# Turning K on VectorE in 32x32 blocks instead of on TensorE, in a decode-attention kernel

## Chip, cores, metric

One NeuronCore of a Trainium2 chip, one launch. The metric is device time in microseconds. The profiled executions give the span, which is about 2 us shorter than that time.

## The reference, cut to what matters

```python
# A: one query token, 32 heads, 4 KV heads, 65,536 cached keys of 128 numbers, bf16
q = (x @ wq).reshape(1, 1, 32, 128)
scores = einsum("bhqd,bhkd->bhqk", q, repeat(k_cache, 8)) * 128 ** -0.5
o = einsum("bhqk,bhkd->bhqd", softmax(scores), repeat(v_cache, 8))
A = o.reshape(1, 1, 4096) @ wo
# B: a small MLP on the same token (w1, w2: 1024x1024; w3: 1024x3584; w4: 3584x1024)
out = x + A + B
```

Almost all bytes are the two caches: 67 MB each of 170 MB. Every byte is used for one token, so there is little arithmetic per byte.

## The kernel before

The caches are cut into 16 units of 16,384 keys. One unit is one K tile and one V tile of 128 partitions x 16,384 bf16 (4.19 MB each). All big loads go through one queue in a fixed order into five rotating buffers; a load is issued when a buffer comes free.

```python
stream = [("wq", 0), ("wq", 1), ("K", 0), ("K", 1), ("V", 0), ("w3", 0), ("w3", 1)]
for u in range(2, NU):
    stream += [("K", u), ("V", u - 1)]
    ...                                   # w1, w2, wo go through one smaller slot
stream += [("V", NU - 1), ("wo", HKV - 1), ("w4", 0), ("w4", 1)]
```

Keys lie on partitions, but the scores contract over the 128 numbers of a key; both kernels turn K for that. Before, TensorE did it, on bf16 pairs read as 4-byte words; VectorE and ScalarE brought the result back to SBUF:

```python
def k_bank(u, b):                         # 16 banks per K tile
    for a in range(4):
        nc.tensor.transpose(pt[:, 128*a:128*(a+1)], words[...], ident_f[:])
    eng = nc.scalar.copy if evac[0] % ACT_EVERY == 0 else nc.vector.tensor_copy
    eng(out=kt[:, 1024*b:1024*(b+1)], in_=pt[:].bitcast(BF16))

def k_scores(u, sub, s):                  # queries padded to 32 columns, four column strips
    for i in range(4):
        for r in range(2):
            nc.tensor.matmul(sc[32*i:32*(i+1), :], lhsT=qpad[:, g, s, r, :],
                             rhs=cols[:, sub, s, :, 32*i:32*(i+1), r], ..., tile_position=(0, 32*i))
    ...                                   # VectorE: scale, maximum; later ScalarE: exp
```

P is then turned by VectorE (`pT`), multiplied with V (`oacc`), and per group of four units merged (`og`, `pm_e`). The end of the program is this:

```python
    compute_w4(0)      # 32 matmuls into psB
    flush()            # the last wo projection: 16 matmuls
    compute_w4(1)      # 24 matmuls
    # cast, then the output is written
```

## Time and profile before

| | before |
|---|---|
| median time | 409.7 us (3 runs, 409.57 to 410.14) |
| busy: PE / DVE / ACT | 275.4 / 207.1 / 108.7 us |
| bytes read | 169.88 MB |

The page of the profile, parts 1 to 3: busy times of the engines; then, in 40 slices of the span, the busy share of the 16 DMA engines in tenths and the rate; then DMA queues as packets, MB and share of all DMA time.

```profile
PE 275.4 (68%) x2420; PEld 196.5 (48%) x2420; DVE 207.1 (51%) x452; ACT 108.7 (27%) x162; POOL 4.6 (1%) x18
...
DMA  8999999999999999999999999999999999999991
GB/s 358 416 444 430 418 425 439 413 424 448 415 444 428 427 416 440 441 423 425 433 438 427 425 422 443 424 428 433 433 435 427 411 451 425 433 420 433 438 402 76
...
q1 hardware_dynamic: 6772, 169.87, 97.5%
q8 instruction: 19, 0.31, 0.3%
q14 instruction: 7, 0.06, 0.0%
```

No engine is near full, but the DMA row is at 9 (90% or more) from the second slice to the last but one. Queue q1 holds the loads. The two "instruction" queues carry the fetches of the program itself: 26 packets, 0.37 MB, for 5706 instructions here. The page gives their share of the same 16 DMA engines (0.3% for q8).

The table of busy time by stretch, for nearly the whole span and for the end (columns: from:to, length, busy time of each engine, granted TensorE clock, DMA share, GB/s):

```profile
4.00:390.00 386.00, 266.06 (x2348) 193.23 (x2349) 206.45 (x451) 107.24 (x160) 2.83 (x5) 0.85 1.00 429
...
396.00:398.00 2.00, 2.00 (x18) 0.69 (x14) 0.00 (x0) 0.00 (x0) 0.00 (x0) 0.77 0.78 317
398.00:400.00 2.00, 2.00 (x22) 0.76 (x18) 0.00 (x0) 0.00 (x0) 0.00 (x0) 1.00 0.56 213
400.00:402.00 2.00, 2.00 (x22) 0.78 (x20) 0.00 (x0) 0.00 (x0) 0.00 (x0) 1.00 0.10 37
```

For 386 us the DMA share is 1.00 at 429 GB/s. At the end the share does not drop at once (0.78, 0.56, 0.10): some DMA engines finish later than others. The sixteen landings that the first part of w4 counts are spread from 389.52 to 394.10 us in the trace's records. The costliest groups of the parts to be replaced (line, engine, operation, output<-inputs, shapes, count | busy, mean ns of one | idle before, and what ended it):

```profile
L366 PE MATMUL ptk<-ident_f,big 128*128 128x128 f32 x1024 | 156.9, 317 | 53.3 <-DMA big<-in_A_k_cache_dram 51.9
...
L370 DVE COPY big<-ptk 128x1024 bf16<-128x1024 bf16 x192 | 126.5, 687 | 83.2 <-PE ptk L366 82.9
L370 ACT COPY big<-ptk 128x1024 bf16<-128x1024 bf16 x64 | 64.7, 1012 | 163.8 <-PE ptk L366 163.7
L381 PE MATMUL sc<-big,qpad 128*32 128x512 bf16 x512 | 42.4, 394 | 17.4 <-ACT big L370 16.5
```

And the end of the chain of waits, in order of time (start us, us, what):

```profile
353.95 40.14 DMA big<-in_B_w_dram
394.14 9.32 PE psB L173 x67
403.48 0.68 DVE out_t L524
```

The first part of w4 lands at 394.14 us. From then on TensorE works through 72 queued matmuls (the chain names 67), and the output follows. The page's chain as a whole also names PE transposes (18% of the span). Those pieces lie where the chain passes through the freeing of a K buffer, while the DMA row beside them is full.

### The profile page before, as it was taken

What the parts mean: (1) busy time and instruction counts of PE and PEld (TensorE: products, weight loads), DVE (VectorE), ACT (ScalarE), POOL (GpSimd) and SP (SyncE); (2) the same over time, 40 slices, a digit from 0 to 9 for tenths busy, and PEclk for the clock granted to TensorE, in tenths of its full rate; (3) what the DMA queues carried; (4) which work ended last, traced back from release to release, by engine and by line L of the source; (5) the groups of instructions that cost most, each with busy time, mean ns of one, the idle gap of its engine ahead of it and who ended that gap; (6) DMA issues with size and microseconds to landing.
All of it is one profiled execution on the core that took longest, in us unless ns stands there. A gap on an engine that the chain in (4) does not pass through costs nothing.

```text
span 407.1 us, 5706 instructions
## 1 busy us (share of the span) xinstructions
PE 275.4 (68%) x2420; PEld 196.5 (48%) x2420; DVE 207.1 (51%) x452; ACT 108.7 (27%) x162; POOL 4.6 (1%) x18
## 2 busy tenths in 40 slices
PE   0377882394677588685858684768695886868346
PEld 0237651272646475455555462646473755656122
DVE  0434771082366656465656393555566654656500
ACT  1011452135034123232322033141411331323100
POOL 1000001000000000000000000000000000000000
PEclk9996997599598959896969899797969696969859
DMA  8999999999999999999999999999999999999991
GB/s 358 416 444 430 418 425 439 413 424 448 415 444 428 427 416 440 441 423 425 433 438 427 425 422 443 424 428 433 433 435 427 411 451 425 433 420 433 438 402 76
DMA packets 7104, 170.27 MB, mean 418 GB/s; under 512 B 1054, under 2 KB 1058, under 8 KB 1446
## 3 DMA queue, kind: packets, MB, share of 16 engines
q1 hardware_dynamic: 6772, 169.87, 97.5%
q8 instruction: 19, 0.31, 0.3%
q14 instruction: 7, 0.06, 0.0%
q0 software_dynamic: 160, 0.02, 0.0%
q10 hardware_dynamic: 146, 0.00, 0.0%
HBM read 169.88 MB, written 0.01 MB: 417 GB/s over the span
## 4 chain that ended last, share of the span: by engine, by line
DMA 62%; PE 30%; DVE 3%; ACT 2%; another core or an unknown queue 1%; issue 1%; SPq 0%
DMA big<-in_A_k_cache_dram 52%; PE ptk L366 18%; DMA big<-in_B_w_dram 10%; PE sc L381 5%; PE psB L173 3%; PE oacc L441 3%; ACT big L370 2%; DVE og L461 1%; PE pm_e L472 1%; DVE big L370 1%; DVE og L459 0%; DVE pT L431 0%; PE pm_mx L403 0%; SPq L132 0%
## 5 line engine op out<-in xcount | busy, mean ns | idle before, releaser
L366 PE MATMUL ptk<-ident_f,big 128*128 128x128 f32 x1024 | 156.9, 317 | 53.3 <-DMA big<-in_A_k_cache_dram 51.9
L366 PEld LDWEIGHTS ptk<-ident_f,big 128*128 128x128 f32 x1024 | 139.9, 165 | 80.3 <-issue 77.3
L370 DVE COPY big<-ptk 128x1024 bf16<-128x1024 bf16 x192 | 126.5, 687 | 83.2 <-PE ptk L366 82.9
L370 ACT COPY big<-ptk 128x1024 bf16<-128x1024 bf16 x64 | 64.7, 1012 | 163.8 <-PE ptk L366 163.7
L381 PE MATMUL sc<-big,qpad 128*32 128x512 bf16 x512 | 42.4, 394 | 17.4 <-ACT big L370 16.5
L390 DVE TENSOR_SCALAR_CACHE_REDUCE s_sb<-sc 128x512 f32<-128x512 f32 x32 | 22.1, 691 | 24.2 <-PE sc L381 23.5
L441 PE MATMUL oacc<-big,pT 128*32 128x512 bf16 x512 | 32.4, 392 | 2.5 <-DMA big<-in_A_v_cache_dram 2.5
L431 DVE STREAM_TRANSPOSE pT<-p_sb 128x512 bf16<-128x512 bf16 x32 | 22.5, 708 | 15.9 <-ACT p_sb L428 15.9
L381 PEld LDWEIGHTS <-qpad 128*32 128x32 bf16 x512 | 12.6, 95 | 28.4 <-issue 18.3
L441 PEld LDWEIGHTS <-pT 128*32 128x32 bf16 x512 | 18.1, 98 | 13.3 <-DVE pT L431 2.5
L472 PE MATMUL pm_e<-og,selbig 128*128 128x128 f32 x32 | 7.8, 422 | 12.9 <-DVE og L461 12.9
L448 ACT COPY ob<-oacc 128x512 f32<-128x512 f32 x12 | 7.0, 585 | 29.9 <-PE oacc L441 29.9
L472 PEld LDWEIGHTS pm_e<-og,selbig 128*128 128x128 f32 x32 | 6.7, 308 | 15.3 <-DVE og L461 11.1
L173 PE MATMUL psB<-big,cols_h 128*1 128x512 bf16 x56 | 7.7, 437 | 5.9 <-DMA big<-in_B_w_dram 5.9
L244 PE MATMUL psh<-big,ln_rep_b 128*32 128x512 bf16 x56 | 5.5, 504 | 7.1 <-DMA big<-in_B_w_dram 7.1
L416 PE MATMUL pm_mx<-ident_f,rep 1*128 1x1 f32 x16 | 3.6, 223 | 9.4 <-DVE rep L408 9.4
L183 PE MATMUL pm_ln<-ln_rowsum_a,ones_f 128*128 128x1 f32 x2 | 0.6, 348 | 13.7 <-DVE ln_rowsum_a L181 13.7
L428 ACT ACTIVATE p_sb<-s_sb,nball_2276 128x512 bf16<-128x512 f32 x8 | 5.7, 714 | 14.5 <-DVE nball_2276 L422 14.5
L461 DVE SCALAR_TENSOR_TENSOR og<-ob,wb,og 128x512 f32<-128x512 f32 x12 | 9.0, 752 | 0.4
L428 ACT ACTIVATE p_sb<-s_sb,nball_1438 128x512 bf16<-128x512 f32 x8 | 5.7, 714 | 12.2 <-DVE nball_1438 L422 12.2
L428 ACT ACTIVATE p_sb<-s_sb,nball_3096 128x512 bf16<-128x512 f32 x8 | 5.7, 715 | 12.0 <-DVE nball_3096 L422 12.0
L416 PEld LDWEIGHTS pm_mx<-ident_f,rep 1*128 1x128 f32 x16 | 2.2, 139 | 12.8 <-DVE rep L408 12.5
(163 smaller groups left out, 111.9 us busy)
## 6 DMA issues: line engine op xcount, KB each, us to landing
big<-in_A_k_cache_dram SPq DMA_DIRECT2D x16, 4096.0 KB, 46.1
big<-in_A_v_cache_dram SPq DMA_DIRECT2D x16, 4096.0 KB, 40.0
big<-in_A_wq_dram SPq DMA_DIRECT2D x2, 4096.0 KB, 21.5
big<-in_B_w_dram SPq DMA_DIRECT2D x2, 3584.0 KB, 40.6
big<-in_B_w_dram SPq DMA_DIRECT2D x1, 4096.0 KB, 40.1
w_624<-in_B_w_dram SPq DMA_DIRECT2D x1, 2048.0 KB, 35.7
w_1109<-in_A_wo_dram SPq DMA_DIRECT2D x1, 2048.0 KB
w_1735<-in_B_w_dram SPq DMA_DIRECT2D x1, 2048.0 KB
```

Source lines behind the costliest of these rows:

```text
L173: nc.tensor.matmul(psB[32 * j:32 * j + 1, :], lhsT=lhsT, rhs=rhs, start=False, stop=False, tile_position=(0, 32 * j), skip_group_check=True)
L366: nc.tensor.transpose(pt[:, 128 * a:128 * (a + 1)], words[:, 512 * b + 128 * a:512 * b + 128 * (a + 1)], ident_f[:])
L370: eng(out=kt[:, 1024 * b:1024 * (b + 1)], in_=pt[:].bitcast(BF16))
L381: nc.tensor.matmul(sc[32 * i:32 * (i + 1), :], lhsT=qpad[:, g, s, r, :], rhs=cols[:, sub, s, :, 32 * i:32 * (i + 1), r], start=(s == 0 and ...
L390: nc.vector.tensor_scalar(out=s_sb[:], in0=sc[:], scalar1=SCALE, scalar2=None, op0=ALU.mult, op1=ALU.max, accum_out=unit[(u, "mx")][:, sub ...
L416: nc.tensor.transpose(pm[:, P:P + 1], unit.pop((u, "rep"))[0:1, :], ident_f[0:1, 0:1])
L428: nc.scalar.activation(out=p_sb[:], in_=s_sb[:], func=ACTF.Exp, bias=nball[:, b:b + 1], scale=1.0, accum_out=lsum[:, sub:sub + 1])
L431: nc.vector.transpose(out=pT[:], in_=p_sb[:])
L441: nc.tensor.matmul(oacc[32 * q:32 * (q + 1), :], lhsT=pT[:, 32 * t:32 * (t + 1)], rhs=vt[:, sub, :, t, :, :], start=(sub == 0 and t < 4), ...
L448: nc.scalar.copy(out=ob[:], in_=oacc[:])
L461: nc.vector.scalar_tensor_tensor(out=og[:], in0=ob[:], scalar=wb[:, k:k + 1], in1=og[:], op0=ALU.mult, op1=ALU.add)
L472: nc.tensor.matmul(pe[:, 0:P], lhsT=selbig[:, cg, :], rhs=og[:, 128 * cg:128 * (cg + 1)], start=(cg == 0), stop=(cg == 3))
```

## The change

The intent: VectorE's transpose, which the kernel before already uses on P (128x512 bf16, 0.71 us), is applied to the 4-byte words of K, in place. The changed kernel assumes that this turns 32x32 blocks and leaves the words of a key on 32 partitions of its own quadrant, four key groups side by side. Query weights that are block-diagonal over the four quadrants then give the scores with the full 128x128 array, and neither TensorE transposes of K nor their evictions remain.

```diff
-    def k_bank(u, b):
-        ... 4 TensorE transposes, 1 eviction on VectorE or ScalarE
+    def k_set(u, sub, s):                       # 8 sets per K tile
+        n = UKEYS // SUBS // SETS
+        at = (SETS * sub + s) * n
+        words = kt[:, at:at + n].bitcast(F32)   # 128 x 1024 words
+        nc.vector.transpose(out=words, in_=words)
+        k_scores(u, sub, s)

     def k_scores(u, sub, s):
-        for i in range(4):
+        for b in range(2):
             for r in range(2):
-                nc.tensor.matmul(sc[32*i:32*(i+1), :], lhsT=qpad[:, g, s, r, :],
-                                 rhs=cols[:, sub, s, :, 32*i:32*(i+1), r], ..., tile_position=(0, 32*i))
+                c0 = LEAD + P * (4 * g + 2 * b + r) - 8 * s
+                nc.tensor.matmul(sc[:], lhsT=qdiag[:, c0:c0 + P], rhs=cols[:, sub, s, :, b, :, r], ...)
@@ cut: query packing for qdiag, layout of V to match, PSUM: 2+2+2 banks instead of 4+1+1 @@
```

More of the change, by code (lines that the diff above doesn't have):

```diff
@@ L19 @@
 SUBS = 2
+SETS = 4
 BIG_BUFS = 5
-ACT_EVERY = 4
 W4_PIECES = (16, 8, 2, 1, 1)
@@ L55 @@
     SCALE = float(DH) ** -0.5
+    LEAD = 8 * (SETS - 1)
     const = ctx.enter_context(tc.tile_pool(name="const", bufs=1))
@@ L67 @@
     dram = ctx.enter_context(tc.tile_pool(name="dram", bufs=1, space=bass.MemoryType.DRAM))
-    ps_T = ctx.enter_context(tc.tile_pool(name="psT", bufs=4, space=bass.MemoryType.PSUM))
-    ps_S = ctx.enter_context(tc.tile_pool(name="psS", bufs=1, space=bass.MemoryType.PSUM))
-    ps_O = ctx.enter_context(tc.tile_pool(name="psO", bufs=1, space=bass.MemoryType.PSUM))
+    ps_T = ctx.enter_context(tc.tile_pool(name="psT", bufs=2, space=bass.MemoryType.PSUM))
+    ps_S = ctx.enter_context(tc.tile_pool(name="psS", bufs=2, space=bass.MemoryType.PSUM))
+    ps_O = ctx.enter_context(tc.tile_pool(name="psO", bufs=2, space=bass.MemoryType.PSUM))
     ps_M = ctx.enter_context(tc.tile_pool(name="psM", bufs=1, space=bass.MemoryType.PSUM))
@@ L157 @@
     nc.gpsimd.memset(eps_t[:], LN_EPS)
-    ones_f = const.tile([P, P], F32, name="ones_f")
+    ones_f = opool.tile([P, P], F32, name="ones_f", tag="ob")
     nc.gpsimd.memset(ones_f[:], 1.0)
@@ L164 @@
     nc.scalar.activation(out=warm_act[:], in_=eps_t[:], func=ACTF.Sqrt)
-    ident_bf = const.tile([P, P], BF16, name="ident_bf")
-    make_identity(nc, ident_bf[:])
-    qpad = const.tile([P, HKV, 2, 2, 32], BF16, name="qpad")
-    nc.gpsimd.memset(qpad[:], 0.0)
+    pick4 = const.tile([P, 4], BF16, name="pick4")
+    nc.gpsimd.tensor_copy(out=pick4[:], in_=ident_f[:, ::32])
+    spread = ogpool.tile([P, 4, P], BF16, name="spread", tag="og")
+    for b in range(2):
+        nc.gpsimd.tensor_copy(
+            out=spread[:, 2 * b:2 * b + 2, :].rearrange("p r (a i) -> p r a i", a=4),
+            in_=ident_f[:, 64 * b:64 * b + 64].rearrange("p (i r) -> p r i", r=2).unsqueeze(2).to_broadcast([P, 2, 4, 32]))
+    qdiag = const.tile([P, LEAD + HKV * 4 * P], BF16, name="qdiag")
+    nc.gpsimd.memset(qdiag[:], 0.0)
     psB = ps_B.tile([P, 512], F32, name="psB")
@@ L228 @@
     nc.vector.tensor_tensor(out=ln_s2[:], in0=negmean1[:], in1=rstd1[:], op=ALU.mult)
-    accx = tmp.tile([1, D], F32, name="accx", tag="t")
-    nc.vector.tensor_scalar(out=accx[:], in0=x_row[:], scalar1=ln_s1[0:1, 0:1], scalar2=ln_s2[0:1, 0:1],
-                            op0=ALU.mult, op1=ALU.add)
     for j in range(2):
-        nc.tensor.matmul(psB[32 * j:32 * j + 32, :], lhsT=first_row[0:1, :], rhs=accx[0:1, 512 * j:512 * (j + 1)],
+        accx = spool.tile([1, 512], F32, name="accx", tag="s_sb")
+        nc.vector.tensor_scalar(out=accx[:], in0=x_row[:, 512 * j:512 * (j + 1)], scalar1=ln_s1[0:1, 0:1],
+                                scalar2=ln_s2[0:1, 0:1], op0=ALU.mult, op1=ALU.add)
+        nc.tensor.matmul(psB[32 * j:32 * j + 32, :], lhsT=first_row[0:1, :], rhs=accx[0:1, :],
                          start=True, stop=False, tile_position=(0, 32 * j), skip_group_check=True)
@@ L262, in compute_wq @@
         del vals["psq"]
-        qpk = tmp.tile([P, 8, 2, 2, 64], BF16, name="qpk", tag="t")
-        for b in range(2):
-            for ts in range(2):
-                eng = nc.vector.tensor_copy if ts == 0 else nc.scalar.copy
-                eng(out=qpk[:, 4 * b:4 * b + 4, :, ts, :],
-                    in_=psq[b][:].rearrange("p (h j r) -> p h r j", h=4, r=2))
-        for r in range(2):
-            pt = ps_T.tile([P, 512], F32, name="ptq", tag="pt")
-            ptb = pt[:].bitcast(BF16).rearrange("p (h x) -> p h x", h=8)
-            for h in range(8):
-                nc.tensor.transpose(ptb[:, h, :], qpk[:, h, r, :, :].rearrange("p t j -> p (t j)"), ident_bf[:])
-            for s in range(2):
-                for ts in range(2):
-                    eng = nc.vector.tensor_copy if s == 0 else nc.scalar.copy
-                    eng(out=qpad[64 * ts:64 * ts + 64, :, s, r, 16 * s + 8 * ts:16 * s + 8 * ts + 8],
-                        in_=ptb[64 * ts:64 * ts + 64, :, ::32].rearrange("p h g -> p g h"))
+        q_row = tmp.tile([P, 2, 512], BF16, name="q_row", tag="t")
+        nc.vector.tensor_copy(out=q_row[:, 0, :], in_=psq[0][:])
+        nc.scalar.copy(out=q_row[:, 1, :], in_=psq[1][:])
+        pq = ps_M.tile([P, 5, 8 * HKV], F32, name="pm_q", tag="pm")
+        for h in range(8):
+            nc.tensor.matmul(pq[:, 4, :].rearrange("p (g h) -> p g h", h=8)[:, :, h],
+                             lhsT=q_row[:, h // 4, P * (h % 4):P * (h % 4 + 1)], rhs=pick4[:], start=True, stop=True)
+        qT = small.tile([P, 8 * HKV], BF16, name="qT")
+        nc.vector.tensor_copy(out=qT[:], in_=pq[:, 4, :])
+        for x in range(4):
+            nc.tensor.matmul(pq[:, x, :], lhsT=spread[:, x, :], rhs=qT[:], start=True, stop=True)
+        for a in range(4):
+            eng = nc.vector.tensor_copy if a % 2 == 0 else nc.scalar.copy
+            at = slice(32 * a, 32 * a + 32)
+            eng(out=qdiag[at, LEAD:].rearrange("p (g x c) -> p x g c", g=HKV, x=4)[:, :, :, 32 * a:32 * a + 8],
+                in_=pq[at, 0:4, :].rearrange("p x (g h) -> p x g h", h=8))
     def to_columns(rows, n, C, tag):
@@ L357 @@
     group = {}
-    evac = [0]
-    def k_bank(u, b):
+    def k_set(u, sub, s):
         kt = st.tiles[("K", u)]
-        words = kt[:].bitcast(F32)
-        pt = ps_T.tile([P, 512], F32, name="ptk", tag="pt")
-        for a in range(4):
-            nc.tensor.transpose(pt[:, 128 * a:128 * (a + 1)], words[:, 512 * b + 128 * a:512 * b + 128 * (a + 1)],
-                                ident_f[:])
-        evac[0] += 1
-        eng = nc.scalar.copy if evac[0] % ACT_EVERY == 0 else nc.vector.tensor_copy
-        eng(out=kt[:, 1024 * b:1024 * (b + 1)], in_=pt[:].bitcast(BF16))
+        n = UKEYS // SUBS // SETS
[3 more added lines that the diff above has]
+        k_scores(u, sub, s)
     def k_scores(u, sub, s):
-        g, b = divmod(u, NB)
+        g = u // NB
         kt = st.tiles[("K", u)]
-        cols = kt[:].rearrange("p (u s t k r) -> p u s t k r", u=SUBS, s=2, t=16, r=2)
+        cols = kt[:].rearrange("p (u s k b x r) -> p u s k b x r", u=SUBS, s=SETS, k=16, b=2, r=2)
         if s == 0:
@@ L378, in k_scores @@
         sc = unit[(u, "sc")]
-        for i in range(4):
+        for b in range(2):
             for r in range(2):
-                nc.tensor.matmul(sc[32 * i:32 * (i + 1), :], lhsT=qpad[:, g, s, r, :],
-                                 rhs=cols[:, sub, s, :, 32 * i:32 * (i + 1), r],
-                                 start=(s == 0 and r == 0), stop=(s == 1 and r == 1), tile_position=(0, 32 * i))
-        if s == 0:
+                c0 = LEAD + P * (4 * g + 2 * b + r) - 8 * s
+                nc.tensor.matmul(sc[:], lhsT=qdiag[:, c0:c0 + P], rhs=cols[:, sub, s, :, b, :, r],
+                                 start=(s == 0 and b == 0 and r == 0), stop=(s == SETS - 1 and b == 1 and r == 1))
+        if s < SETS - 1:
             return
@@ L388, in k_scores @@
             unit[(u, "ssb")] = []
-        s_sb = spool.tile([P, 512], F32, name="s_sb")
+        s_sb = spool.tile([P, 512], F32, name="s_sb", tag="s_sb")
         nc.vector.tensor_scalar(out=s_sb[:], in0=sc[:], scalar1=SCALE, scalar2=None, op0=ALU.mult, op1=ALU.max,
@@ L406, in max_row @@
                                 op=ALU.max, negate=True)
-        rep = small.tile([1, P], F32, name="rep")
+        rep = small.tile([1, P], F32, name="rep", bufs=1)
         nc.vector.tensor_copy(out=rep[:].rearrange("o (j h) -> o j h", h=8),
@@ L435, in compute_v @@
         g, b = divmod(u, NB)
-        vt = st.tiles[("V", u)][:].rearrange("p (u s t k d) -> p u s t k d", u=SUBS, s=2, t=16, k=2)
+        vt = st.tiles[("V", u)][:].rearrange("p (u s t d) -> p u s t d", u=SUBS, s=SETS, t=16)
         oacc = ps_O.tile([P, 512], F32, name="oacc")
@@ L441, in compute_v @@
                 nc.tensor.matmul(oacc[32 * q:32 * (q + 1), :], lhsT=pT[:, 32 * t:32 * (t + 1)],
-                                 rhs=vt[:, sub, :, t, :, :], start=(sub == 0 and t < 4),
+                                 rhs=vt[:, sub, :, t, :], start=(sub == 0 and t < 4),
                                  stop=(sub == SUBS - 1 and t >= 12), tile_position=(0, 32 * q))
@@ L453, in compute_v @@
         lall = group.pop((g, "lall"))
-        og = ogpool.tile([P, 512], F32, name="og")
+        og = ogpool.tile([P, 512], F32, name="og", tag="og")
         negmg = small.tile([P, 1], F32, name="negmg")
@@ L474, in group_rows @@
         nc.tensor.matmul(pe[:, P:P + 1], lhsT=sel8big[:], rhs=lp[:, 0:1], start=True, stop=True)
-        msk = small.tile([P, 16, 8], F32, name="msk")
+        msk = small.tile([P, 16, 8], F32, name="msk", bufs=1)
         nc.vector.tensor_tensor(out=msk[:], in0=pe[:, 0:P].rearrange("p (dd j) -> p dd j", j=8),
@@ L491, in group_project @@
         st.done(("wo", g))
-    BANKS = UKEYS // P // 8
     def compute_k(u):
-        for b in range(BANKS):
-            k_bank(u, b)
-            if b % 4 == 3:
-                after(2, lambda sub=b // 8, s=(b // 4) % 2: k_scores(u, sub, s))
-            tick()
+        for sub in range(SUBS):
+            for s in range(SETS):
+                k_set(u, sub, s)
+                tick()
     for it in stream:
```

## The prediction

> **What bounds the kernel now.** The DMA queue. The page's DMA table gives the load queue 97.5% of the 16 engines' span for 169.87 MB. The table of busy time by stretch shows DMA share 0.98 to 1.01 and 422 to 435 GB/s in every stretch from 4 us to 390 us, whether PE works (74% of 300 to 340 us: 430 GB/s) or not (4 to 10 us: 426). [...] A K load lands 46.1 us after issue (table of DMA issues): four to five tiles of 4.19 MB stand in the queue, so the queue never runs dry although the SP queue waits 220 us for DVE to free K buffers. Outside the load stream lie about 3 us of start and a tail: loads fade between 396 and 400 us, then 24 w4 matmuls (2.75 us), a cast (0.68 us), the output write, end at 407.1.
>
> The chain of waits names PE transposes (18%) and scores (5%), but beside a full DMA queue; they do not set the time.
>
> **Removed.** 1024 PE transposes (156.9 us busy), their PSUM evictions: 192 on DVE (126.5 us, 687 ns each) and 64 on ACT (64.7 us); 512 score matmuls on 32-column strips (42.4 us).
>
> **Added.** 128 DVE transposes in place of 128x1024 words. The trace's 128x512 bf16 transpose takes 0.71 us; [...] No run so far shows that a 4-byte element keeps that rate. And 512 full-array score matmuls over 512 columns: V's 32 strip matmuls run in 1.73 us, four side by side, so 0.216 us per 512 columns at full clock: estimate 111 us, up to twice that at half clock.
>
> **Balance.** DVE: 207 - 126.5 + 159, about 240 us (59%). PE: 275 - 199 + 111 to 160, about 190 to 235 us. ACT about 44 us. Per K+V pair the DMA needs 8.39 MB / 0.43 = 19.5 us; DVE needs 8 x 1.24 plus about 3.7 us of score eviction, P transposes and small work, about 13.6 us; PE some 9 to 14 us. Everything stays below the DMA.
>
> **On the critical path: nearly nothing.** The same bytes at the same rate, and the same tail, since PE idles before w4 in both. Predicted time 409.5 us, 80% range 406.5 to 412.5. Chances: faster by over 2% 0.02, within 2% 0.91, slower by over 2% 0.07.
>
> **What the profile would show.** Right: DMA queue again 97 to 98%, 415 to 421 GB/s mean; transposes near 1.24 us, DVE 56 to 62%, ACT near 11%, PE down to 45 to 60%; w4's first part still lands near 394 us. Transposes of about 2.3 us would refute the rate. A DMA share falling in mid-span would refute the bound.
>
> **What would make it wrong.** (1) 4-byte transposes at half rate: then DVE needs 8 x 2.3 + 3.7 = 22 us per pair, over the 19.5 of the DMA, and the time becomes some 415 to 425 us. (2) DVE's in-place traffic slowing DMA writes into the same memory; a 1% lower rate costs 4 us. (3) DVE's order: transposes of the next K behind a group merge that waits for V, draining the queue; 46 us of backlog should absorb it. (4) Faster than 402 us would need a load rate over 437 GB/s or no tail at all.

The step from the measured 0.71 us to the time of the new transpose came to 1.24 us each and 159 us for 128, the terms that stand under "Balance" (207 - 126.5 + 159, about 240 us; 8 x 1.24 + 3.7, about 13.6 us per pair); the 2.3 us for half rate rests on it too. These are guesses, for the run to test. The 409.5 us is the time before with the same loads and the same tail; the terms enter it only in that 13.6 us stays under the 19.5 us of the loads. The 437 GB/s of (4) works out as 169.87 MB in 402 us less about 13 us of start and tail.

## The result, and the profile after

| | before | after |
|---|---|---|
| median time | 409.68 us (4 runs, 409.57 to 410.14) | 408.75 us (4 runs, 407.91 to 408.94) |
| busy: PE / DVE / ACT | 275.4 / 207.1 / 108.7 us | 245.6 / 226.7 / 43.0 us |
| instructions | 5706 | 3502 |

The ratio is 0.9971, with a 95% interval of 0.9954 to 0.9989: the same at 2%, yet faster by a small amount that is clear of noise. Two later repeats gave 0.9969 and 0.9968. A ratio here is the mean time of one kernel's fast runs over that of the other's of the same rounds, so not quite the ratio of the medians quoted.

The same views of the changed kernel. The page, parts 1 to 3:

```profile
PE 245.6 (60%) x1392; PEld 97.6 (24%) x1392; DVE 226.7 (56%) x387; ACT 43.0 (11%) x95; POOL 6.4 (2%) x19
...
DMA  9999999999999999999999999999999999999991
GB/s 361 413 454 418 418 443 426 420 424 446 419 446 422 429 420 438 436 435 415 441 432 419 440 419 437 432 432 429 437 420 432 425 433 435 436 425 417 448 401 56
...
q1 hardware_dynamic: 6772, 169.87, 97.5%
q8 instruction: 11, 0.18, 0.2%
...
q14 instruction: 5, 0.04, 0.0%
```

Its table of busy time by stretch:

```profile
4.00:390.00 386.00, 235.51 (x1320) 94.20 (x1321) 226.04 (x386) 41.48 (x93) 2.95 (x6) 0.80 1.00 430
...
396.00:398.00 2.00, 2.00 (x14) 0.69 (x12) 0.00 (x0) 0.00 (x0) 0.00 (x0) 0.62 0.78 304
398.00:400.00 2.00, 2.00 (x22) 0.79 (x20) 0.00 (x0) 0.00 (x0) 0.00 (x0) 1.00 0.29 104
400.00:402.00 2.00, 2.00 (x22) 0.83 (x20) 0.00 (x0) 0.00 (x0) 0.00 (x0) 1.00 0.00 0
```

The groups that took the place of the four shown of the kernel before:

```profile
L387 PE MATMUL sc<-big,qdiag 128*128 128x512 bf16 x512 | 150.5, 457 | 82.5 <-DVE big L374 82.2
L374 DVE STREAM_TRANSPOSE big<-big 128x1024 f32<-128x1024 f32 x128 | 147.9, 1212 | 60.0 <-DMA big<-in_A_k_cache_dram 60.0
```

The end of its chain of waits:

```profile
350.62 42.39 DMA big<-in_B_w_dram
393.06 10.13 PE psB L182 x72
403.21 0.68 DVE out_t L526
```

What the reader should see: TensorE lost 30 us, ScalarE 66 us, VectorE gained 20 us, and the load queue did not notice: share 1.00, 430 GB/s instead of 429. VectorE now waits for K loads directly (60.0 us). The one difference on the path is at the end: the first part of w4 lands at 393.06 us, 1.08 us earlier (393.24 and 393.14 us in two repeats of the changed kernel), and the fade of the loads ends before 400 us instead of after it. Part of that is given back, because TensorE stayed at a granted clock of 0.50 longer in the tail (mean 0.62 instead of 0.77 from 396 to 398 us; the first 32 matmuls took 5.80 us instead of 4.98), so the two profiled spans differ by 0.3 us only, while the medians of the timed runs differ by 0.9 us.

### The profile page after: what moved, and what is told of

The parts are those of the page before. It is cut to its first block, busy times and chain, and to the rows that moved or that the text cites. A ratio compares the mean times of both kernels' runs of the same rounds, so it can differ in the third digit from the quotient of the medians.

```text
span 406.8 us, 3502 instructions
## 1 busy us (share of the span) xinstructions
PE 245.6 (60%) x1392; PEld 97.6 (24%) x1392; DVE 226.7 (56%) x387; ACT 43.0 (11%) x95; POOL 6.4 (2%) x19
## 3 DMA queue, kind: packets, MB, share of 16 engines
q1 hardware_dynamic: 6772, 169.87, 97.5%
## 4 chain that ended last, share of the span: by engine, by line
DMA 62%; PE 26%; DVE 10%; issue 1%; another core or an unknown queue 0%; SPq 0%; DVEq 0%
DMA big<-in_A_k_cache_dram 51%; PE sc L387 16%; DMA big<-in_B_w_dram 10%; DVE big L374 5%; PE oacc L446 4%; PE psB L182 3%; DVE s_sb L395 2%; DVE og L466 1%; PE pm_e L477 1%; PE pm_mx L408 0%; DVE pT L436 0%; DVE og L464 0%; PE pm_mx L421 0%; DVE rep L413 0%
## 5 line engine op out<-in xcount | busy, mean ns | idle before, releaser
L387 PE MATMUL sc<-big,qdiag 128*128 128x512 bf16 x512 | 150.5, 457 | 82.5 <-DVE big L374 82.2
L374 DVE STREAM_TRANSPOSE big<-big 128x1024 f32<-128x1024 f32 x128 | 147.9, 1212 | 60.0 <-DMA big<-in_A_k_cache_dram 60.0
L387 PEld LDWEIGHTS <-qdiag 128*128 128x128 bf16 x512 | 57.3, 112 | 175.7 <-issue 83.0
L446 PE MATMUL oacc<-big,pT 128*32 128x512 bf16 x512 | 42.9, 491 | 4.8 <-DMA big<-in_A_v_cache_dram 4.8
L395 DVE TENSOR_SCALAR_CACHE_REDUCE s_sb<-sc 128x512 f32<-128x512 f32 x32 | 21.6, 674 | 19.9 <-PE sc L387 19.9
L446 PEld LDWEIGHTS <-pT 128*32 128x32 bf16 x512 | 15.0, 115 | 22.2 <-issue 16.0
L408 PE MATMUL pm_mx<-ident_f,mxb 128*1 128x128 f32 x16 | 4.3, 269 | 16.6 <-DVE mxb L401 16.6
L182 PE MATMUL psB<-big,cols_h 128*1 128x512 bf16 x56 | 8.6, 472 | 5.3 <-DMA big<-in_B_w_dram 5.3
L192 PE MATMUL pm_ln<-ln_rowsum_a,ones_f 128*128 128x1 f32 x2 | 0.6, 348 | 13.6 <-DVE sel_180 L216 13.6
L464 DVE TENSOR_SCALAR og<-oacc,wb 128x512 f32<-128x512 f32 x4 | 3.0, 748 | 9.2 <-PE oacc L446 9.2
L481 DVE TENSOR_TENSOR msk<-pm_e,mask_188 128x128 f32<-128x128 f32 x4 | 1.2, 291 | 12.2 <-PE pm_e L479 12.2
```

The source lines that it names most:

```text
L182: nc.tensor.matmul(psB[32 * j:32 * j + 1, :], lhsT=lhsT, rhs=rhs, start=False, stop=False, tile_position=(0, 32 * j), skip_group_check=True)
L374: nc.vector.transpose(out=words, in_=words)
L387: nc.tensor.matmul(sc[:], lhsT=qdiag[:, c0:c0 + P], rhs=cols[:, sub, s, :, b, :, r], start=(s == 0 and b == 0 and r == 0), stop=(s == SETS ...
L395: nc.vector.tensor_scalar(out=s_sb[:], in0=sc[:], scalar1=SCALE, scalar2=None, op0=ALU.mult, op1=ALU.max, accum_out=unit[(u, "mx")][:, sub ...
L408: nc.tensor.transpose(pm[0:1, 0:P], unit.pop((u, "mxb"))[:, 0:1], ident_f[:])
L446: nc.tensor.matmul(oacc[32 * q:32 * (q + 1), :], lhsT=pT[:, 32 * t:32 * (t + 1)], rhs=vt[:, sub, :, t, :], start=(sub == 0 and t < 4), sto ...
```

## The experiments

One warning first. The comparison with the reference cannot vouch for attention in this problem. Kernels below that leave attention out altogether were also called correct, so its part of the output lies within the tolerance. That the changed layout is right was checked only by following its indices.

Theory: the load queue sets the time; all engine work of either kernel fits beside it. Rivals: VectorE or TensorE work is partly on the path, as the chain of waits suggests; or engine traffic in SBUF slows the loads.

### 1. Loads without attention

```diff
     def compute_k(u):
-        ... transposes, scores
+        nc.vector.tensor_copy(out=touch[:], in_=st.tiles[("K", u)][:, UKEYS - 2:])
+        st.done(("K", u))
     # compute_v likewise; wo is projected from zeros
```

> The changed kernel without any attention arithmetic: every K and V tile is still loaded, but only touched by one tiny VectorE copy (result wrong on purpose). If the load queue alone sets the time: 406.5 to 409 us, about 430 GB/s from 4 to 390 us, the 32 KB packets as long as before. Rival, that engine traffic in the memory slows the loads: a rate near 435 GB/s and 404.5 us or less.

Measured: 405.58 us (404.93 to 405.67), ratio to before 0.9887. (The rival's 435 GB/s is also the highest stretch in the prediction's table of the kernel before, 220 to 260 us.) The table by stretch of this run:

```profile
4.00:390.00 386.00, 40.94 (x240) 13.86 (x241) 11.74 (x69) 4.57 (x9) 2.90 (x6) 0.56 1.00 430
```

The queues of this run (page, part 3):

```profile
q8 instruction: 2, 0.03, 0.0%
...
q14 instruction: 2, 0.02, 0.0%
```

The end of its TensorE timeline (start us, us, what):

```profile
391.57 8.52 PE L182 MATMUL psB<-big,cols_h 128*1 128x512 bf16 x56 [6.14 <-DMA big<-in_B_w_dram]
```

With VectorE busy 12 us instead of 226, the rate is the same 430 GB/s. The 32 KB packets of the loads took 1220 ns on average, against 1221 ns in the kernel before and in the changed one (from the packet records in the traces, which no view prints). That refutes the rival of memory traffic. The time is nevertheless 1 us below what the theory had, and 3 us below the changed kernel. The trace shows where: the last wo projection no longer stands in the tail (56 matmuls after the first w4 landing instead of 72), and w4 lands at 391.57 us, 1.5 us earlier than in the changed kernel. The rate as printed (whole GB/s) is too coarse to show the latter. There is something small that grows with the program, and experiment 5 follows it.

### 2. How much VectorE work fits: 32 and 128 more transposes

```diff
         nc.vector.transpose(out=words, in_=words)
+        if s == 0:                                   # two_more; without the condition: twice
+            nc.vector.transpose(out=words, in_=words)
```

> The changed kernel with one extra transpose in 2 of the 8 sets of every K tile: 32 more transposes, 38 us more VectorE work (result wrong on purpose). My theory: VectorE's chain per K+V pair is about 16 to 17 us in the trace of after, 2.4 us more is 19 us, still under the 19.5 us of the loads: 408 to 411 us. Rival, that VectorE work lies on the critical path as the chain of waits shows (5%): some of the 38 us must show, 412 us or more.

Measured: 408.15, 408.26 and 408.45 us in three runs, ratio 0.9957. The added VectorE work (32 transposes of 1.2 us, about 38 us) cost nothing that shows. The profiled execution of this kernel fell into a state of 758 us and is not used, so no trace shows where the added work went.

> Every K set transposed twice: 128 more transposes, 154 us more VectorE work (result wrong on purpose), which is also what a transpose at half rate would have cost. Theory: VectorE's serial chain per pair becomes about 16 + 9.6 = 25.6 us, over the 19.5 us of the loads; 32 us start + 16 x 25.6 + about 20 us = 460 us (425 to 475). If only VectorE's busy time counted, 23.1 us per pair: about 416 us, as the prediction had it. If all of the added work lay on the critical path: 563 us.

Measured: 475.64 us (473.66 to 476.93), ratio 1.1595. The page of twice, parts 1 and 3:

```profile
PE 270.2 (57%) x1392; PEld 96.5 (20%) x1392; DVE 370.6 (78%) x515; ACT 40.7 (9%) x93; POOL 6.4 (1%) x19
...
q1 hardware_dynamic: 6772, 169.87, 84.3%
```

What VectorE waited for in it, beside loads (us in total, times, longest us):

```profile
DVE s_sb L396 <- PE sc L388: 29.2, 23, 1.9
DVE pT L437 <- ACT p_sb L434: 15.2, 15, 2.5
...
DVE negm L411 <- PE pm_mx L409: 8.9, 15, 1.1
```

Of 154 us expected, and 144 us of added busy time (370.6 - 226.7), 67 us show. The load share fell to 84%, so here VectorE sets the pace. Its chain of one unit took 25.1 us in the timeline (transposes of one K tile starting at 322.76 us, of the next at 347.86), against 25.6 expected and 19.5 us of loads per pair; over all 16 units it is 25.8 us ((445.0 - 32.4) / 16). The time was 0.6 us above the top of the stated range. What matters more: the prediction had costed just this case ("4-byte transposes at half rate") at 415 to 425 us from busy time alone. The busy sum, which ignores waits, was 50 to 60 us short: VectorE also waits for the last scores, for exp and for the maximum before it may go on, 53 us in the three lines above.

### 3. The arithmetic alone

Two K tiles and one V tile are loaded once and then used for all 16 units, in both kernels.

```diff
+                slot = (kind, i % 2 if kind == "K" else 0)
+                if slot in self.kept:
+                    self.tiles[it] = self.kept[slot]
+                    return                              # no load
```

> The kernel before with two K tiles and one V tile loaded once and used for all 16 units (result wrong on purpose): only the arithmetic sets the time. At full TensorE clock PE needs about 12 us per pair (64 transposes 7.6, scores 2.6, V 1.7) and VectorE 12.0: expected 13 us per pair, 32 + 16 x 13 + 20 = 260 us (245 to 285).

> The changed kernel, K and V kept in the same way (result wrong on purpose). VectorE's chain is about 16 us per pair, as in the trace of after: 32 + 16 x 16 + 20 = 308 us (285 to 320), so slower than the kernel before without its loads: the change buys no arithmetic capacity. Rival: the change makes the arithmetic lighter (PE 275 to 246 us, 5706 to 3502 instructions) and the loads hide it: then faster than the kernel before without loads by 10% or more.

(The 7.6, 2.6 and 1.7 us are from the trace of the kernel before at a granted clock of 0.99 to 1.00: 16 transposes in 1.90 us, 8 score matmuls in 0.65, V's 32 in 1.73.)

Measured: before 286.98 us (286.81 to 287.31; 2 us above my range), after 271.2 us (269.21 to 271.84; 14 us below it). My theory fell: the changed kernel is faster here, by 5.5%, about half of what the rival asked for. One stretch of the table by stretch, of the kernel before with kept tiles:

```profile
120.00:140.00 20.00, 19.99 (x212) 12.81 (x208) 15.34 (x33) 9.82 (x16) 0.00 (x0) 1.00 0.29 106
```

And one of the changed kernel with kept tiles:

```profile
180.00:200.00 20.00, 17.10 (x108) 6.05 (x106) 19.75 (x33) 3.62 (x9) 0.00 (x0) 1.00 0.00 1
```

Without loads to wait for, the kernel before is bound by TensorE (19.99 of 20 us busy), the changed one mostly by VectorE (19.75 of 20). Over the nine stretches of 20 us from 60 to 240 us the means are 19.2 us for TensorE before, and after it 19.2 us for VectorE with TensorE close behind at 18.2, so the second bound is less clear than in the stretch shown. From the first K work to the last, one unit takes 14.2 us before ((260.5 - 32.5) / 16) and 13.1 us after ((242.4 - 32.3) / 16). I had taken the 16 to 17 us chain of the changed kernel's trace for its capacity; but that chain held waits. In the kept kernel the build put the P transposes between the K transposes of the next unit, and most of the waits vanished (VectorE waited 6.8 us for scores in the whole run, against 19.9 us in the changed kernel). So the change does buy arithmetic capacity, 16 us in all; both kernels need 13 to 14 us per unit where the loads need 19.5, and the gain is hidden behind the load queue.

### 4. The tail, in both kernels

```diff
-    compute_w4(0)
-    flush()
+    flush()                # the last wo projection first
+    compute_w4(0)
     compute_w4(1)
-    w4 part 0: one load of 16 pieces
+    w4 part 0: two loads of 8 pieces
```

> The changed kernel once more, for comparison in the same rounds: 408 to 409 us, ratio to before 0.996 to 0.9985.

> The changed kernel with the last projection of attention put ahead of w4 and the first w4 load in two halves, so that less TensorE work is left when the last bytes land. If what lies outside the load stream is the only other time to win: 1.5 to 3 us less than the changed kernel, 405.5 to 407.3 us. Rival, the last landing alone sets the end: no change.

> The same tail in the kernel before: 1.5 to 3 us less, 406.5 to 408.2 us; the two gains add, and the tail is worth more than the change.

Measured in the same rounds: changed kernel again 408.91 us (ratio 0.9969), changed kernel with the new tail 406.65 us (ratio 0.9924, interval 0.9908 to 0.9939), kernel before with the new tail 408.36 us (ratio 0.9961, interval 0.9945 to 0.9977; its median lies 0.16 us above the range that I gave). The changed kernel with the new tail is the best version found. The timeline of its TensorE shows why:

```profile
388.31 3.58 PE L182 MATMUL psB<-w,oT 128*1 128x512 bf16 x16 [1.06 <-DVE oT L488]
391.67 4.13 PE L182 MATMUL psB<-big,cols_h 128*1 128x512 bf16 x32
398.04 2.96 PE L182 MATMUL psB<-big,cols_h 128*1 128x512 bf16 x24 [2.23 <-DMA big<-in_B_w_dram]
```

The wo projection now runs while w4 is still under way, and TensorE even waits 2.23 us for the last pieces. By medians the new tail gave 2.3 us to the changed kernel and 1.8 us to the kernel before, and rebuilding the K path 1.3 us; by the ratios it is about 1.8, 1.6 and 1.3 us. The runs of both kernels with the new tail fall into two groups about 1.4 us apart, and the intervals of the tail alone (0.9945 to 0.9977) and of the change alone (0.9957 to 0.9981) overlap, so that the tail is worth more than the change is not shown. The new tail is also two edits, the order and the split load, which were not tried apart.

### 5. The small gain: instruction fetches?

The changed kernel fetches 16 instruction packets instead of 26, the kernel without attention 4, and w4 lands at 393.06, 394.14 and 391.57 us: in the same order. To test it, tiny memsets on the idle GpSimd bring the instruction count back.

```diff
         k_scores(u, sub, s)
+        for _ in range(18):
+            nc.gpsimd.memset(idle[:], 0.0)
```

> The changed kernel with 2304 tiny memsets on the otherwise idle GpSimd: about as many instructions as the kernel before (some 141 KB more to fetch, 8 to 10 more packets of 16 KB that the same DMA engines carry). If the small gain of the change comes from fewer instruction fetches among the loads: 0.5 to 1.2 us slower than the changed kernel, ratio to before 0.9985 to 1.001. Rival, the gain comes from elsewhere (tail, TensorE clock, memory traffic): same as the changed kernel, 0.996 to 0.998.

(The 141 KB can be worked out from the two pages: 0.37 MB for 5706 instructions and 0.22 MB for 3502, about 64 bytes each; 16 KB is q8's 0.31 MB over 19 packets.)

Measured: 417.04 us, ratio 1.017. This run does not answer the question. 594 memsets stood ahead of the small transfers that GpSimd issues for w2 and w4 (the first went out at 92 us instead of 64), and in one of the 40 slices the load rate fell to 147 GB/s. So it was repeated with the memsets behind those transfers (their first input is the last transfer's output), and with a control in which 352 longer memsets keep GpSimd about as busy (188 us, against 213).

```diff
+        if u >= 5:                                   # pad_late: 26 memsets of 2 elements
+            for _ in range(26):                      # pad_few: 4 memsets of 512 elements
+                nc.gpsimd.memset(idle[:], 0.0)
```

> The changed kernel once more beside the two padded ones: ratio to before 0.996 to 0.998, instruction fetches 0.22 MB, the first part of w4 lands near 393 us.

> The first padded run starved the load queue, because the tiny memsets stood ahead of the small GpSimd transfers that w2 and w4 need. Here 2288 tiny memsets follow after those transfers: about 0.36 MB of instructions fetched, as in the kernel before, and no starved queue. If fewer fetches are the gain of the change: first part of w4 lands near 394 us, ratio to before 0.9985 to 1.0005. Rival, the gain comes from elsewhere: 393 us and 0.996 to 0.998.

> Control: GpSimd kept busy for as long (about 190 us) by 352 longer memsets, so almost nothing more is fetched. Under the fetch theory like the changed kernel, 0.996 to 0.998; if GpSimd's work itself slows the loads, like the other padded run.

Measured in the same rounds: changed kernel 408.32 us (0.9968), pad_few 408.74 us (0.9972), pad_late 432.37 us (1.0544). The time of pad_late is no measure: its memsets themselves ran until 429 us. Its landings are. The instruction queues on the page of pad_late:

```profile
q8 instruction: 11, 0.18, 0.2%
q14 instruction: 23, 0.19, 0.1%
```

Its table by stretch, at the end of the loads:

```profile
398.00:400.00 2.00, 0.00 (x0) 0.00 (x0) 0.00 (x0) 0.00 (x0) 1.22 (x14) 0.50 0.23 90
400.00:402.00 2.00, 1.67 (x10) 0.49 (x11) 0.00 (x0) 0.00 (x0) 1.23 (x14) 0.50 0.06 20
402.00:404.00 2.00, 2.00 (x16) 0.73 (x14) 0.00 (x0) 0.00 (x0) 1.21 (x14) 0.71 0.06 25
404.00:406.00 2.00, 2.00 (x22) 0.78 (x18) 0.00 (x0) 0.00 (x0) 1.24 (x14) 1.00 0.09 35
406.00:408.00 2.00, 2.00 (x22) 0.80 (x20) 0.00 (x0) 0.00 (x0) 1.20 (x14) 1.00 0.06 23
```

The first matmuls on w4 in the changed kernel of the same rounds, in pad_few and in pad_late (start us, us, what):

```profile
393.14 5.30 PE L182 MATMUL psB<-big,cols_h 128*1 128x512 bf16 x32 [6.12 <-DMA big<-in_B_w_dram]
393.20 6.55 PE L182 MATMUL psB<-big,cols_h 128*1 128x512 bf16 x32 [5.30 <-DMA big<-in_B_w_dram]
400.33 5.00 PE L182 MATMUL psB<-big,cols_h 128*1 128x512 bf16 x32 [5.98 <-DMA big<-in_B_w_dram]
```

18 more packets of 8 KB than in the changed kernel (16 of them before 393 us) moved the first landing of w4 from 393.14 to 400.33 us, 7.2 us, although 0.15 MB at 430 GB/s would be 0.35 us. The fetch theory had the direction right, but its 394 us was 6 us too early. The share column says how: from 400 us on it is 0.06, one sixteenth (0.09 from 404 to 406 us, where a packet of q8 is fetched as well). That is what one DMA engine of the sixteen gives that is still busy with its part of the loads while the others are done. The landing records in the trace, which no view prints, show it directly: each load counts sixteen landings, and for the first part of w4 fifteen of them came from 389.43 to 392.89 us and the sixteenth at 400.29 us, just before TensorE began. So the load was complete only when its slowest engine was, 7.4 us after the others. That the extra packets ran on just this engine is inferred: the 16 took about 0.31 us each, 5 us in all. In the control, which fetched 19 packets, w4 landed at 393.20 us, as in the changed kernel, so it is the fetching and not GpSimd's work. (The control is not perfect: its memsets ended at 301 us.)

So added fetches do delay the last landing (400.33 us, against 393.20 in the control), and the change saves ten of them. How much of the gain of 0.3% that is, the packet records answer in part. As a mean over the 16 engines, the instruction packets took 1.41 us in the kernel before and 0.84 us in the changed one; the packets of the loads took 396.91 and 396.74 us. So 0.57 of the 0.74 us that the engines saved are fetches, and the sixteen landings of w4's first part came 0.80 us earlier on average (391.88 and 391.08 us). This is an account, not an experiment: the ten saved packets are mostly on queue q8, the added ones all on q14, and nothing here isolated q8. That fetches are all of the gain is not shown.

## Why the prediction was right, point by point

- **The bound.** Right. 97.5% and 418 GB/s mean again, and 430 GB/s with the engines nearly idle (experiment 1).
- **"On the critical path: nearly nothing."** Right to 0.3%. The predicted 409.5 us was 0.75 us above the median. "The same tail" and "the same bytes" were not quite right: w4 landed 1.08 us earlier, with ten fewer instruction packets on the same DMA engines.
- **VectorE's transpose.** Guessed at 1.24 us, measured 1.21 (mean). Words of 4 bytes in place took no longer for each than elements of 2 bytes: 1203 ns (median) for 128x1024 words of K in the changed kernel, 1.17 ns per column, against 711 ns for 128x512 elements of P in the kernel before, 1.39 ns per column. What of that is a fixed part and what a rate, two sizes of two types do not show. Predicted VectorE busy "about 240 us", measured 226.7: back-to-back transposes overlap a little (128 x 1.21 = 155 us summed, 147.9 busy).
- **TensorE.** The score matmuls came to 150.5 us, inside the 111 to 160 us. One started every 0.22 us at a granted clock of 1.00 (18 from 363.7 to 367.4 us) and every 0.43 us at 0.50 (13 from 340.8 to 345.9 us): the 0.216 us and the "twice" of the prediction. V's strip matmuls, its "four side by side", started every 0.05 us (32 from 58.4 to 59.9 us in the kernel before, at 379 ns each). The sum, "about 190 to 235", was 245.6: mis-sized was the rest, which was assumed unchanged. V's matmuls went from 32.4 to 42.9 us, 10.5 of the 19 us by which the rest was off, while the mean granted clock fell from 0.85 to 0.80. At 353 us, for example, V's 32 matmuls ran at a clock of 0.50 to 0.56 and took 3.24 us; in the kernel before they ran at 1.00 and took 1.96 us. At the start of the K tile at 340 us the clock stood at 0.50 until about 346 us in both kernels, and only then at 1.00. In the changed kernel that was about 5 us after the first score matmul (340.80 us), and 3 us in its next K tile (360.17 to about 363.2 us). The miss cost no time, because TensorE is not on the path.
- **What would make it wrong, (1).** Not met, but its price was mis-sized: "415 to 425 us" for 22 us per pair. Experiment 2 gave 476 us, because VectorE's serial order makes 25 us of it. Neither (2) nor (3) came: the load share stayed at 1.00 and the rate at 430 GB/s.

## What to carry to other kernels

Before costing a change, look at whether one resource is at 1.00 in every stretch; if so, only its bytes, its rate, or the time before its start and after its end can move, and a rewrite that takes 66 us off one engine and 30 us off another is worth what those three are worth (here 0.9 of 409.7 us). Look for the cheap gain in what is left to do after the last landing: here a new order and a split load gave as much as the rewrite, or more. And cost an overloaded engine from its serial chain with its waits, not from its busy sum, and not from a chain that contains waits for loads when you want its capacity.
